# Query features in a linear-attention and FFN kernel: the eighth head pair in the empty rows of the seven others, the seventh pair in one group of 64x64 tiles

## The chip, the cores and the metric

The kernel runs on one core of one Trainium2 chip. The metric is the device time of one execution in microseconds (us). PE is TensorE, PEld its weight loads, ACT is ScalarE, DVE is VectorE, POOL is GpSimd and SP is SyncE, which issues most DMAs. A pair `p` of sequence tiles is 256 rows (there are 8: `NPAIR`); a head pair is two of the 16 heads (also 8).

## The reference

One layer norm feeds a linear attention with softmax feature maps and a SiLU FFN; both are added to the input. The sequence has 2048 rows, the width is 448, there are 16 heads of 28 and the FFN is 1792 wide.

```python
xn = _layernorm(x, axis=-1)
return x + _A_ref(xn, A_wqkv, A_w_phi, A_wo) + _B_ref(xn, B_w1, B_w2)
...
q, k, v = qkv[0], qkv[1], qkv[2]
pq = jnp.einsum("bhsd,hdf->bhsf", q, w_phi)
pk = jnp.einsum("bhsd,hdf->bhsf", k, w_phi)
phi_q = jnp.concatenate([_softmax(pq, axis=-1), _softmax(-pq, axis=-1)], axis=-1)
phi_k = jnp.concatenate([_softmax(pk, axis=-1), _softmax(-pk, axis=-1)], axis=-1)
kv = jnp.einsum("bhsf,bhsd->bhfd", phi_k, v)
z  = jnp.einsum("bhsf->bhf", phi_k)
num = jnp.einsum("bhqf,bhfd->bhqd", phi_q, kv)
den = jnp.einsum("bhqf,bhf->bhq", phi_q, z)[..., None] + 1e-6
...
h = _silu(jnp.einsum("bsd,df->bsf", x, w1))
out = jnp.einsum("bsf,fd->bsd", h, w2)
```

## The kernel before

All work is recorded as operations of a small planner (`P.op`, `P.dma`), each with an estimated duration; `schedule` simulates the five engines and fixes for each the order of its instructions. Data dependencies become semaphore waits (a DMA has a semaphore of its own), `odeps` only fix an order on one engine. In the attention and output stages the order of PE is written out by hand in the list `chain`. All matmuls go out through two helpers, so the profile shows them under few lines: L446 (`mms`, matmuls), L459 (`trs`, transposes), L465 (`act`, all of ACT), L469 (`copy_dve`).

The contraction over 448 is cut into rows of 64: `contract` issues steps of two matmuls, one on array rows 0 to 63 and one on rows 64 to 127, into two neighbouring PSUM banks for the two sequence tiles; a first pass of 4 steps and a second pass of 3 steps, which begins after the first has ended.

The stages in order of time:

1. Layer norm, transposes of the normed input into `xnT`, and the first layer of the FFN for the first part of the sequence (`ffn1_single`, `ffn1_chunk`, SiLU on ACT), from 0 to about 41 us. In between `fold(kt)` (L795), for four row blocks `kt`, multiplies the query and key weights by `w_phi` into banks 6 and 7 and copies the result to `wqk_sb`, where each head pair has 56 columns and 8 columns of padding. For the queries the padding is set to zero by a POOL memset (L526).
2. Attention, pair by pair, 41 to 84 us. `k_macro(p)` (L877) computes key features (`pk_mm`, 14 matmuls), two exponentials of them on ACT (`exp_k`), the values (`v_mm`, banks 2 and 3, copied by DVE as `v_ev`), sums `Sk`, reciprocals `Rk` on DVE, and the product `phik`, mostly on POOL (L900). `q_group(ch, c)` (L922), one for each `p`, computes the query features of two head pairs (2c and 2c+1) for one half of the sequence (`ch`, 1024 rows) as 7 steps of 512 columns into banks 6 and 7. The output has 128 rows: 56 of the first head pair, 8 empty, 56 of the second, 8 empty. Two exponentials (`exp_q`, plus and minus) write them to `EqT`. `k_acc(p)` accumulates the key-value product in bank 4, in odd pairs from the third on, between the two passes of the q group.
3. The rest of FFN layer 1, the transposed key-value block `KVZ` (`kv_transpose`), and the first `q_products` (`U_mm`): for one pair of sequence tiles, each of the four column blocks `c` of `EqT`, rows 0 to 55 and 64 to 119, times `KVZ`.
4. From 93.5 us on, `out_pair(p)`: FFN layer 2 and the output projection into one pair of banks (`obank`), `q_products(p + 2)` and `q_divide(p + 2)` (DVE, L1016 to L1029; POOL, L1051) in between, then the store.

```python
        for p in range(NPAIR):
            k12, v12 = k_macro(p)
            q12 = q_group(p // 4, p % 4)
            if p > 1 and p % 2:
                chain += [k12[0], v12[0], k12[1], v12[1], q12[0], k_acc(p - 3), k_acc(p - 2), q12[1]]
            else:
                chain += [k12[0], v12[0], k12[1], v12[1][:2], q12[0], v12[1][2:], q12[1]]
```

The memory `EqT` holds `[128 rows, 4 column blocks c, 2 signs, 2 sequence tiles, 1024]`; the first of its blocks serves as scratch in stage 1.

Of the kernel before, what the change touches and what calls it, by code (L numbers as in the profile page):

```python
# [8 lines left out]
ACTF = mybir.ActivationFunctionType  # L9
# [323 lines left out]
def bass_parallel_sum__linear_kernel_hedgehog__dense_activation_silu__prompt_kernel(  # L333
# [11 lines left out]
    NT, NPAIR = S // 128, S // 256  # L345
    KF = 3
    FT = FF // 128
# [7 lines left out]
    with es:  # L355
# [6 lines left out]
        xnT = sb("xnT", [128, 8, NPAIR, 128], BF16)  # L362
        wqk_sb = sb("wqk_sb", [128, 4, 2, 8, 64], BF16)
# [56 lines left out]
        P = _Prog()  # L420
        UP, LO = slice(0, 64), slice(64, 128)

        def d_mm(n):
            return max(n * 0.4167 + 1.0, 55.0)
# [4 lines left out]
        def d_dve(n, mode=1):  # L429
            return n * 1.042 / mode + 150.0  # L430
# [4 lines left out]
        def d_pool(n, per=1.0):  # L435
            return n * per + 120.0
# [27 lines left out]
        def act(dst, src, func, name, table=None, scale=1.0):  # L464
            return P.op("act", d_act(_cols(src)), lambda e: e.activation(dst, src, func, scale=scale),  # L465
                        reads=[src], writes=[dst], table=table, name=name)

        def copy_dve(dst, src, name, dur):
            return P.op("dve", dur, lambda e: e.tensor_copy(dst, src), reads=[src], writes=[dst], name=name)  # L469

        def xb(par, k):
            return 3 if k == 3 else (k if par == 0 else 4 + k)

        def contract(jobs, n, first, last, name, sync=None):

            passes = ([((0, 0, UP), (1, 0, LO)), ((0, 1, UP), (1, 1, LO)), ((0, 2, UP), (1, 2, LO)), ((0, 3, UP), (1, 3, LO))],
                      [((0, 0, LO), (1, 0, UP)), ((0, 1, LO), (1, 1, UP)), ((0, 2, LO), (1, 2, UP))])
            prev, done = None, []  # L480
            for q, steps in enumerate(passes):
                ops = []
                for X, W, dsts, opens, wstat in jobs:
                    for i, step in enumerate(steps):
                        parts = []
                        for par, k, r in step:
                            xx, ww = X(r, xb(par, k)), W(r, k)
                            lhsT, rhs = (ww, xx) if wstat else (xx, ww)
                            parts.append((dsts[par], lhsT, rhs, first and opens and q == 0 and i == 0,
                                          last and q == 1 and i == len(steps) - 1))  # L490
                        ops.append(mms(parts, name, d_mm(n)))
                if q == 1:
                    for o in ops:
                        o.syncs.add(prev.id)
                prev = ops[-1]
                done.append(ops)
            return done
# [24 lines left out]
            P.op("pool", d_pool(16, 2.0), lambda e: e.tensor_copy(kvz1, mask2[:, None, :].broadcast_to([128, 8, 2])),  # L522
                 reads=[mask2[:]], writes=[kvz1], name="kvz1")

        qpad = wqk_sb[:, :, 0, :, 56:64]
        P.op("pool", d_pool(256, 0.9), lambda e: e.memset(qpad, 0.0), writes=[qpad], name="qpad")  # L526
        P.op("pool", d_pool(256, 0.9), lambda e: e.memset(wraw[:, :, 2 * D:], 0.0), writes=[wraw[:, :, 2 * D:]], name="wpad")
        def warm(n, cols=256):

# [245 lines left out]

        def exp_act(dst, src, scale, name):
            o = act(dst, src, ACTF.Exp, name, table="exp", scale=scale)
            for s in silus:
                if s.id not in o.deps:
                    o.odeps.add(s.id)  # L780
            exps.add(o.id)
# [13 lines left out]
        def fold(kt):  # L795
            bA, bB = banks[6], banks[7]
            for w in range(9):
                parts = []
                pairs = [(UP, 4, bA, 448)] if w == 0 else [(UP, (w - 1) % 4, bA, 56 * (w - 1))]
                if 1 <= w <= 7:  # L800
                    pairs.append((LO, w % 4, bB, 56 * (w - 1)))
                for r, g, bk, c in pairs:
                    parts.append((bk[:, c:c + 56], wT[r, w, 128 * kt:128 * kt + 128], BD[r, g, :], True, True))
                mms(parts, "fold_mm", 36.0)
            qk = wqk_sb[:, kt].rearrange("p s (c j) u -> p (s c) j u", j=2)
            for src, dst, eng in ((bA[:, 0:448], qk[:, :, 1, 0:56], "act"), (bB[:, 0:392], qk[:, 1:8, 0, 0:56], "dve"),
                                  (bA[:, 448:504], qk[:, 0, 0, 0:56], "act")):
                n = _cols(src)
                if n > 56:
                    src = src.rearrange("p (s u) -> p s u", u=56)  # L810
                if eng == "act":
                    act(dst, src, ACTF.Identity, "fold_ev")
                else:
                    copy_dve(dst, src, "fold_ev", d_dve(n))

        ev0, order0 = lnz_first()
        banks_ = iter((0, 2, 4, 0, 2, 4, 0, 2))
# [58 lines left out]

        def k_macro(p):  # L877
            sl = p % NEK
            kbk = 4 if p == 1 else 0
            k12 = proj(p, lambda r, k: wqk_sb[r, k, 1, :, 0:56], kbk, "pk_mm")  # L880
            kb = psum[:, kbk * 512:kbk * 512 + 1024].rearrange("p (t c) -> p t c", t=2)[:, :, 0:D]
            for s in range(2):
                exp_act(Ek[sl][:, :, s * D:(s + 1) * D], kb, 1.0 if s == 0 else -1.0, "exp_k")
            v12 = proj(p, lambda r, k: wv_sb[r, k, :], 2, "v_mm")
            vb = psum[:, 1024:2048].rearrange("p (t c) -> p t c", t=2)[:, :, 0:D].rearrange("p t (h d) -> p t h d", h=H)
            copy_dve(vaug[sl][:, :, :, 0:DH], vb, "v_ev", d_dve(896))
            for t0, t1 in ((0, 2),) if p < NPAIR - 1 else ((0, 1), (1, 2)):
                n = t1 - t0
                E4 = Ek[sl][:, t0:t1, 0:2 * D].rearrange("p t (h f) -> p t h f", f=DH)
                S3, R3 = Sk[:, sl, 32 * t0:32 * t1], Rk[:, sl, 32 * t0:32 * t1]  # L890
                S4, R4 = (a.rearrange("p (t h) -> p t h", t=n) for a in (S3, R3))
                P.op("dve", d_dve(896 * n), lambda e, S4=S4, E4=E4: e.tensor_reduce(S4, E4, AXL.X, ALU.add),  # L892
                     reads=[E4], writes=[S3], name="Sk")
                P.op("dve", d_rec(32 * n), lambda e, S3=S3, R3=R3: e.reciprocal(R3, S3), reads=[S3], writes=[R3], name="Rk")
                for s0, s1, eng in ((0, 2, "pool"),) if t0 == 0 else ((0, 1, "dve"), (1, 2, "pool")):
                    h0, h1 = 16 * s0, 16 * s1
                    E5, R5 = E4[:, :, h0:h1], R4[:, :, h0:h1]
                    R5 = R5[:, :, :, None].broadcast_to([128, n, h1 - h0, DH])
                    P.op(eng, 1100 if eng == "dve" else d_pool(448 * n * (s1 - s0), 1.72),
                         lambda e, E5=E5, R5=R5: e.tensor_tensor(E5, E5, R5, ALU.mult),  # L900
                         reads=[E5, R5], writes=[E5], name="phik")

            return k12, v12
# [16 lines left out]
            return ops  # L920

        def q_group(ch, c):  # L922
            done = contract([(lambda r, b: xnT[r, b, 4 * ch:4 * ch + 4, :].rearrange("p a c -> p (a c)"),
                       lambda r, k: wqk_sb[r, k, 0, 2 * c:2 * c + 2, :].rearrange("p j u -> p (j u)"),
                       [banks[6 + par] for par in range(2)], True, True)], 512, True, True, "pq_mm")
            src = psum[:, 6 * 512:8 * 512].rearrange("p (r c) -> p r c", r=2)
            for s in range(2):
                exp_act(EqT[:, c, s, :, ch * 512:(ch + 1) * 512], src, 1.0 if s == 0 else -1.0, "exp_q")
            return done

        for sl in range(NEK):
            P.op("pool", d_pool(32), lambda e, sl=sl: e.memset(vaug[sl][:, :, :, DH], 1.0),
                 writes=[vaug[sl][:, :, :, DH]], name="vaug1")
        P.cur_prio = 0
        chain = []
        for p in range(NPAIR):
            k12, v12 = k_macro(p)
            q12 = q_group(p // 4, p % 4)
            if p > 1 and p % 2:
                chain += [k12[0], v12[0], k12[1], v12[1], q12[0], k_acc(p - 3), k_acc(p - 2), q12[1]]  # L940
            else:
                chain += [k12[0], v12[0], k12[1], v12[1][:2], q12[0], v12[1][2:], q12[1]]
        kv = k_acc(NPAIR - 2) + k_acc(NPAIR - 1)
        ready = [o.id for o in P.ops if o.name == "phik"][-2:]
        for o in kv:
# [39 lines left out]
        U4 = psum[:, UB * 512:UB * 512 + 2048].rearrange("p (q c) -> p q c", q=4)[:, :, 0:480].rearrange("p q (h c) -> p q h c", c=DZ)  # L985

        def obank(p):
            return 6 if p % 2 == 0 else 0

        def q_products(p):  # L990
            for t in range(2):
# [133 lines left out]

        unit_no[0] = 0
        k = len(units_done)
        ffn1_chunk(4, 2, 12, FT, (0,))
        unit_no[0] = 0
        ffn1_chunk(6, 2, 0, FT, (2, 6, 0, 6, 0, 6, 0))  # L1130
        u = units_done[k:]
        uu = []
        for p in range(2):
# [128 lines left out]
```

## Time and profile before

| | |
|---|---|
| three timed runs | 157.41, 156.87, 156.2 us (median 156.87) |
| profiled execution, its own time | 156.01 us |
| its span, first to last instruction | 154.3 us |
| PE busy | 149.6 us (97%) |
| DVE, ACT, POOL busy | 99.6, 75.7, 55.0 us |
| granted TensorE clock | 0.998 |
| q matmuls (64x512) | 112, 14.8 us busy |
| exponentials into EqT | 16 of 1.02 us |

A line of the chain of waits or of the timeline gives the start in us, the length in us, the engine, the line of the source and the number of instructions; a line of the waits gives who waited for whom, us in total, times, and the longest. The busy time of PE includes the modelled tail of each matmul, so costs of steps are read from the starts of consecutive groups.

### The profile page before, as it was taken

What the parts mean: (1) busy time and instruction counts of PE and PEld (TensorE: products, weight loads), DVE (VectorE), ACT (ScalarE), POOL (GpSimd) and SP (SyncE); (2) the same over time, 40 slices, a digit from 0 to 9 for tenths busy, and PEclk for the clock granted to TensorE, in tenths of its full rate; (3) what the DMA queues carried; (4) which work ended last, traced back from release to release, by engine and by line L of the source; (5) the groups of instructions that cost most, each with busy time, mean ns of one, the idle gap of its engine ahead of it and who ended that gap; (6) DMA issues with size and microseconds to landing.
All of it is one profiled execution on the core that took longest, in us unless ns stands there. A gap on an engine that the chain in (4) does not pass through costs nothing.

```text
span 154.3 us, 5662 instructions
## 1 busy us (share of the span) xinstructions
PE 149.6 (97%) x2576; PEld 98.9 (64%) x2576; DVE 99.6 (65%) x177; ACT 75.7 (49%) x89; POOL 55.0 (36%) x79
## 2 busy tenths in 40 slices
PE   6999999999998999999999999999999999999992
PEld 4698889898743445454478886645565555555672
DVE  1969788862427989494994597675665748393203
ACT  3586775569779886869869566021020202022000
POOL 7021123020100788858395024642516060605000
PEclk9999999999999999999999999999999999999999
DMA  4967754000004331210000000001101010101012
GB/s 129 339 190 185 256 170 130 4 4 4 4 0 121 123 119 59 79 44 0 4 0 4 4 0 6 4 0 64 46 18 59 0 64 0 64 2 64 0 64 60
DMA packets 8629, 9.60 MB, mean 62 GB/s; under 512 B 1501, under 2 KB 8221, under 8 KB 8605
## 3 DMA queue, kind: packets, MB, share of 16 engines
q1 hardware_dynamic: 8140, 8.96, 18.6%
q8 instruction: 20, 0.33, 0.9%
q10 hardware_dynamic: 464, 0.28, 0.6%
q14 instruction: 5, 0.03, 0.1%
HBM read 7.37 MB, written 1.84 MB: 60 GB/s over the span
## 4 chain that ended last, share of the span: by engine, by line
PE 94%; ACT 3%; issue 1%; POOL 0%; DVE 0%; ACTq 0%; POOLq 0%
PE psum L446 90%; PE psum L459 3%; ACT EqT L465 1%; ACT L465 1%; ACT scr L465 1%; ACT xnT L465 0%; DVE out_sb L1080 0%; POOL ident L501 0%; PE psum L967 0%; POOL ones_bf L500 0%; POOL neghalf L504 0%; ACTq L1202 0%; POOLq L1247 0%; POOL ones L505 0%
## 5 line engine op out<-in xcount | busy, mean ns | idle before, releaser
L446 PE MATMUL psum<-xnT,w_sb 64*128 64x256 bf16 (+1 forms) x768 | 46.8, 268 | 0.1
L446 PE MATMUL psum<-w_sb,hT 64*128 64x448 bf16 (+2 forms) x504 | 46.6, 328 | 0.0
L446 PEld LDWEIGHTS psum<-xnT,w_sb 64*128 64x128 bf16 x768 | 35.3, 94 | 5.2 <-PE psum L446 0.7
L465 ACT ACTIVATE hT<-psum 128x1024 bf16<-128x1024 f32 (+1 forms) x29 | 28.3, 995 | 13.8 <-PE psum L446 13.2
L1051 POOL TENSOR_TENSOR xn_sb<-wraw 128x448 bf16<-128x448 f32 (+4 forms) x39 | 20.7, 562 | 37.0 <-DVE wraw L1029 37.0
L446 PEld LDWEIGHTS psum<-w_sb,hT 64*128 64x128 bf16 x504 | 22.7, 94 | 16.6 <-ACT oT L465 0.4
L465 ACT ACTIVATE oT<-psum 128x896 bf16<-128x896 bf16 x8 | 7.3, 917 | 40.4 <-PE psum L459 40.4
L900 POOL TENSOR_TENSOR scr<-scr,Rk 128x1792 bf16<-128x1792 bf16 x6 | 19.3, 3211 | 18.0 <-ACT scr L465 11.3
L465 ACT ACTIVATE EqT<-psum 128x1024 bf16<-128x1024 f32 x16 | 15.5, 1023 | 5.5 <-PE psum L446 5.5
L1029 DVE TENSOR_TENSOR wraw<-psum,Gq 128x1792 f32<-128x1792 f32 (+1 forms) x9 | 16.4, 1817 | 0.9
L446 PE MATMUL psum<-xnT,wqk_sb 64*128 64x512 bf16 x112 | 14.8, 378 | 0.4 <-ACT EqT L465 0.4
L1080 DVE TENSOR_TENSOR out_sb<-psum,x_sb 128x896 bf16<-128x896 f32 (+2 forms) x9 | 8.8, 981 | 9.5 <-PE psum L446 9.4
L1016 DVE RECIPROCAL R<-psum 128x64 f32<-128x64 f32 (+1 forms) x9 | 4.6, 512 | 14.9 <-PE psum L446 14.9
L446 PE MATMUL psum<-wv_sb,xnT 64*128 64x448 bf16 x112 | 14.0, 349 | 0.0
L446 PE MATMUL psum<-wo_sb,oT 64*128 64x448 bf16 (+2 forms) x126 | 13.6, 328 | 0.0
L446 PE MATMUL psum<-wqk_sb,xnT 64*128 64x448 bf16 x112 | 13.2, 349 | 0.0
L607 DVE BATCH_NORM_STATS2 st<-x_sb 128x6 f32<-128x448 bf16 x16 | 9.8, 615 | 4.4 <-DMA x_sb<-in_A_x_dram 4.4
L892 DVE TENSOR_REDUCE Sk<-scr 128x64 f32<-128x1792 bf16 x6 | 12.1, 2013 | 0.6 <-ACT scr L465 0.6
L616 POOL TENSOR_TENSOR rstd<-ve,neghalf 128x2 f32<-128x2 f32 (+1 forms) x8 | 5.4, 670 | 19.6 <-DVE ve L615 19.6
L469 DVE CAST scr<-psum 128x896 bf16<-128x896 f32 x6 | 6.5, 1083 | 8.9 <-PE psum L446 8.9
L465 ACT ACTIVATE scr<-psum 128x896 bf16<-128x896 f32 x12 | 10.4, 922 | 0.7 <-PE psum L446 0.4
L446 PEld LDWEIGHTS psum<-xnT,wqk_sb 64*128 64x128 bf16 x112 | 4.7, 94 | 6.9 <-PE psum L446 1.7
(69 smaller groups left out, 139.6 us busy)
## 6 DMA issues: line engine op xcount, KB each, us to landing
out_dram<-out_sb SPq DMA_DIRECT2D x7, 224.0 KB, 1.9
w_sb<-in_B_w_dram SPq DMA_DIRECT2D x3, 448.0 KB, 3.3
x_sb<-in_A_x_dram SPq DMA_DIRECT2D x2, 448.0 KB, 4.3
w_sb<-in_B_w_dram SPq DMA_DIRECT2D x2, 384.0 KB, 7.2
x_sb<-in_A_x_dram SPq DMA_DIRECT2D x3, 224.0 KB, 6.1
w_sb<-in_B_w_dram SPq DMA_DIRECT2D x3, 224.0 KB, 3.3
wraw<-in_A_wqkv_dram SPq DMA_DIRECT2D x1, 672.0 KB, 4.8
w_sb<-in_B_w_dram SPq DMA_DIRECT2D x1, 576.0 KB, 4.2
```

The source lines that it names most:

```text
L446: r = e.matmul(dst, lhsT, rhs, start=start, stop=stop, skip_group_check=True)
L459: out = e.transpose(dst, src, ident[r, 64:128] if r == LO else ident[r, 0:64])
L465: return P.op("act", d_act(_cols(src)), lambda e: e.activation(dst, src, func, scale=scale), reads=[src], writes=[dst], table=table, name= ...
L469: return P.op("dve", dur, lambda e: e.tensor_copy(dst, src), reads=[src], writes=[dst], name=name)
L607: P.op("dve", 600, lambda e: e.bn_stats(st6[:, t, :], x_sb[:, t, :]), reads=[x_sb[:, t, :]], writes=[st6[:, t, :]], name="bnst")
L616: P.op("pool", 580, lambda e: e.tensor_tensor(r2, v2, nh, ALU.pow), reads=[v2, nh], writes=[r2], name="rstd")
L892: P.op("dve", d_dve(896 * n), lambda e, S4=S4, E4=E4: e.tensor_reduce(S4, E4, AXL.X, ALU.add), reads=[E4], writes=[S3], name="Sk")
L900: lambda e, E5=E5, R5=R5: e.tensor_tensor(E5, E5, R5, ALU.mult),
L1016: P.op("dve", d_rec(32 * n), lambda e, R3=R3, U=U: e.reciprocal(R3, U[:, :, :, DH + 1]), reads=[U[:, :, :, DH + 1]], writes=[r2], name="R2")
L1029: P.op("dve", d_dve(896 * n), lambda e, dsto=dsto, U=U, G3=G3, n=n: e.tensor_tensor(dsto, U[:, :, :, 0:DH], G3[:, :, :, None].broadcast_to ...
L1051: lambda e, dst=dst, a0=a0, a1=a1: e.tensor_tensor(dst, a0, a1, ALU.add),
L1080: P.op("dve", d_dve(2 * (c1 - c0)), lambda e: e.tensor_tensor(dst, ob, xs, ALU.add), reads=[ob, xs], writes=[dst], name="out_ev")
```

## The change

The zero padding of the query weights goes. In `fold`, the 56 query columns of the eighth head pair are also copied, 8 at a time, into the 8 padding columns of the seven other head pairs, and the copies of the fold change engines. So every q product now yields, in the 8 rows that were empty, 8 of the eighth pair's features.

Six `q_group`s remain (three for each half of the sequence, head pairs 0 to 5). In pair 3 a new `q_half` computes the seventh head pair for both halves of the sequence at once: each step has four matmuls on 64x64 tiles, two row halves times two halves of the sequence, the latter in rows 0 to 63 and 64 to 127 of the output. Pair 5 has no q group. DMAs within SBUF (`q_move`, issued on SP) then bring the features where `q_products` reads them: one of 56 rows (224 KB) and fourteen of 8 rows (32 KB each).

The banks of the q and k products in some pairs, of two FFN units and of the output pairs change; a dummy exponential (`pre_exp`) is placed after the last SiLU ahead of the attention's exponentials; the last four `Sk`/`Rk` operations get a fixed order.

As built, the order of instructions changes on PE also in the fold: 32, 24 (of them 2 a little later) and 24 FFN matmuls of 256 columns stand between the folds, and more behind the last. On SP two of the DMAs stand ahead of the three loads of `wo`, thirteen behind them and ahead of the stores. The first `U_mm` of the fourth column block waits for 7 DMA semaphores in pair 0 and for 8 in pair 4.

```diff
-        qpad = wqk_sb[:, :, 0, :, 56:64]
-        P.op("pool", d_pool(256, 0.9), lambda e: e.memset(qpad, 0.0), writes=[qpad], name="qpad")
...
         def exp_act(dst, src, scale, name):
             o = act(dst, src, ACTF.Exp, name, table="exp", scale=scale)
+            o.odeps.add(pre_exp.id)
...
-            for src, dst, eng in ((bA[:, 0:448], qk[:, :, 1, 0:56], "act"), (bB[:, 0:392], qk[:, 1:8, 0, 0:56], "dve"),
-                                  (bA[:, 448:504], qk[:, 0, 0, 0:56], "act")):
+            for src, dst, eng in ((bA[:, 0:448], qk[:, :, 1, 0:56], "dve"), (bB[:, 0:392], qk[:, 1:8, 0, 0:56], "act"),
+                                  (bA[:, 448:504], qk[:, 0, 0, 0:56], "dve")):
...
+            copy_dve(wqk_sb[:, kt, 0, 0:7, 56:64], bA[:, 168:224].rearrange("p (g u) -> p g u", u=8), "fold_ev", d_dve(56))
...
-            kbk = 4 if p == 1 else 0
+            kbk = {1: 4, 2: 6, 6: 6, 7: 6}.get(p, 0)
...
         def q_group(ch, c):
+            qb = {1: 0, 2: 4, 5: 0, 6: 0}.get(4 * ch + c, 6)
...
-                       [banks[6 + par] for par in range(2)], True, True)], 512, True, True, "pq_mm")
-            src = psum[:, 6 * 512:8 * 512].rearrange("p (r c) -> p r c", r=2)
+                       [banks[qb + par] for par in range(2)], True, True)], 512, True, True, "pq_mm")
+            src = psum[:, qb * 512:(qb + 2) * 512].rearrange("p (r c) -> p r c", r=2)
...
+        def q_half():
+            qb, done = 6, []
+            for q in range(2):
+                ops = []
+                for k in range(KF + 1 - q):
+                    parts = []
+                    for h, r in enumerate((UP, LO)):
+                        t = h if q == 0 else 1 - h
+                        for ch in range(2):
+                            parts.append((banks[qb + t][64 * ch:64 * ch + 64, :], wqk_sb[r, k, 0, 6, :],
+                                          xnT[r, xb(t, k), 4 * ch:4 * ch + 4, :].rearrange("p a c -> p (a c)"),
+                                          q == 0 and k == 0, q == 1 and k == KF - 1))
+                    ops.append(mms(parts, "pq_mm", d_mm(512), 65))
+                done.append(ops)
+            for o in done[1]:
+                o.syncs.add(done[0][-1].id)
+            src = psum[:, qb * 512:(qb + 2) * 512].rearrange("p (r c) -> p r c", r=2)
+            for s in range(2):
+                exp_act(EqT[:, 3, s, :, 0:512], src, 1.0 if s == 0 else -1.0, "exp_q")
+            return done
+
+        def q_move(dp, sp, n, c, dch, sch, name):
+            dst = EqT[dp:dp + n, 3, :, :, dch * 512:dch * 512 + 512]
+            src = EqT[sp:sp + n, c, :, :, sch * 512:sch * 512 + 512]
+            P.dma(lambda e: e.dma_start(out=dst, in_=src), n * 4096, reads=[src], writes=[dst], name=name)
+
+        def q_last(ch):
+            for g in range(6):
+                q_move(64 + 8 * g, 56 + 64 * (g % 2), 8, g // 2, ch, ch, "q_last")
...
+        pre_exp = act(pre[:, 1:2], neghalf[:, 0:1], ACTF.Exp, "pre", "exp")
+        pre_exp.odeps.update(o.id for o in silus)
+        exps.add(pre_exp.id)
...
-            q12 = q_group(p // 4, p % 4)
-            if p > 1 and p % 2:
+            q12 = []
+            if p == 3:
+                q12 = q_half()
+                q_move(112, 120, 8, 3, 1, 0, "q_last")
+                q_move(0, 64, 56, 3, 1, 0, "q_half")
+                q_move(112, 56, 8, 3, 0, 0, "q_last")
+                q_last(0)
+            elif p != 5:
+                q12 = q_group(p // 4, p % 4 - (p > 5))
+            if p == NPAIR - 1:
+                q_last(1)
+            if p == 5:
+                chain += [k12[0], v12[0], k12[1], v12[1], k_acc(2), k_acc(3)]
+            elif p > 1 and p % 2:
...
+        sums = [o for o in P.ops if o.name in ("Sk", "Rk")][-4:]
+        for a, c in zip(sums, sums[1:]):
+            c.odeps.add(a.id)
...
-            return 6 if p % 2 == 0 else 0
+            return 0 if p % 2 == 0 else 6
...
-        ffn1_chunk(4, 2, 12, FT, (0,))
+        ffn1_chunk(4, 2, 12, FT, (6,))
...
-        ffn1_chunk(6, 2, 0, FT, (2, 6, 0, 6, 0, 6, 0))
+        ffn1_chunk(6, 2, 0, FT, (2, 0, 6, 0, 6, 0, 6))
```

## The prediction

> **What bounds the kernel now.** I read the page's head first, then the chain that ended last, then the waits of TensorE (PE), then the timeline of the attention middle (41 to 84 us), which is where the change lies.
>
> ```profile
> span 154.3 us, 5662 instructions
> ...
> PE 149.6 (97%) x2576; PEld 98.9 (64%) x2576; DVE 99.6 (65%) x177; ACT 75.7 (49%) x89; POOL 55.0 (36%) x79
> ...
> PE 94%; ACT 3%; issue 1%; POOL 0%; DVE 0%; ACTq 0%; POOLq 0%
> ...
> PE psum L446 <- POOL ones L505: 1.4, 1, 1.4
> PE psum L446 <- ACT EqT L465: 0.4, 1, 0.4
> ```
>
> PE is busy 97% of the span and owns 94% of the chain that ended last. Its matmuls have two idle spells that the waits name: 1.4 us at the start, and 0.4 us behind an exponential into EqT. So only two things are worth time: matmul steps taken off PE, and that 0.4 us. The chain shows where the second comes from:
>
> ```profile
> 44.02 1.28 ACT L465
> ...
> 45.31 0.89 ACT scr L465 x2
> ...
> 46.92 1.96 ACT EqT L465 x2
> ...
> 48.93 36.54 PE psum L446 x496
> ```
>
> Between 44.0 and 48.9 the chain runs through ScalarE (ACT): its table load (1.28 us), exp_k of pair 0, exp_q of pair 0, and then PE again. The second q group needs banks 6 and 7, which exp_q of pair 0 is still reading. The next lines give the price of one q group and of a change of tile shape:
>
> ```profile
> 57.55 1.03 PE L446 MATMUL psum<-xnT,wqk_sb 64*128 64x512 bf16 x8
> ...
> 58.51 0.98 PE L446 MATMUL psum<-scr 128*58 128x112 bf16 x32
> ...
> 59.41 0.82 PE L446 MATMUL psum<-xnT,wqk_sb 64*128 64x512 bf16 x6
> ...
> 60.07 0.92 PE L446 MATMUL psum<-wqk_sb,xnT 64*128 64x448 bf16 x8
> ...
> 62.53 1.03 PE L446 MATMUL psum<-xnT,wqk_sb 64*128 64x512 bf16 x8
> ...
> 63.39 0.35 PE L446 MATMUL psum<-wv_sb,xnT 64*128 64x448 bf16 x2
> ```
>
> The printed length of a group includes the pipeline's tail, so I take starts. At 62.53 eight matmuls (four steps of two row halves) hold PE until 63.39: 0.86 us, 0.215 us for a step of 512 columns, or 0.42 ns a column.
>
> **The change part by part.**
>
> *Fewer steps.* Before, eight q groups take 7 steps each, 56 in all. After, six groups of that kind remain (42 steps), and q_half takes 7 steps of four 64x64 tiles for the seventh head pair in both halves of the sequence. The eighth pair's 56 features ride in the 8 empty columns of each of the seven others and cost no step. If four tiles take one step's time, 7 steps go: 7 x 0.215 = 1.50 us, all from the bounding engine. No row of before has four tiles at once. The neighbours are two: the q steps run two row halves together, and the kv matmuls (58.51) run two column halves together: 32 of 112 columns one after the other would be 32 x 47 ns = 1.49 us, and they take 0.90. Bounds for the seven steps: 0.215 us each (four together), 0.43 (two together: gain 0), 0.86 (one by one: 3.0 us lost). I take 0.215, since both kinds of pairing are in the trace and their product is what is asked for. The Trainium skill, "TensorE: Matmul & The Clock Gate", section "Part 3: Packing small matmuls — row/col tiling", gives about 4 ns for each further tile of a pack; by that the seven steps would take 7 x 3 x 4 ns = 0.08 us more, an estimate that no run here shows.
>
> *The idle spell.* After, the second q group takes banks 0 and 1, which exp_k of pair 0 left at 47.04, so PE need not wait at 48.5: 0.40 us. The table load is also pulled forward by a dummy exponential that follows the last silu (end 42.91) instead of waiting for the first k product; exp_k would start at 42.91 + 1.28 + 0.2 = 44.4 instead of 45.31. That alone would also free bank 6 before 48.5, so the two edits are worth 0.40 together, not 0.40 each. Bounds 0.3 and 0.41.
>
> *Changes of tile shape.* At 58.51 PE goes from 64x128 tiles to 128x64. Four steps from 57.55 end at 58.41, so the change costs 0.10; the way back costs 0.90 - 16 x 0.047 = 0.15. Today this is one round trip in each odd pair from the third on. With q_half, pair 3 goes 64x128, 64x64, 128x64, 64x64, 64x128: two changes more, 0.10 to 0.15 each. I take 0.20; bounds 0 (the row halves are kept) and 0.50. The Trainium skill says the same as the row in "TensorEngine Tiling (Array Packing)", section "Key Properties": changing the mode drains the array, changing the tile does not. By that rule all four changes of pair 3 are paid in full, and the trace agrees for the two that it has.
>
> *Waits on the copies.* U_mm of the fourth column block now reads rows brought by DMA: 7 semaphores at the first pair, 8 more at the fifth. If they are long met, only the queue's handling counts. For fold_mm at 32 us PE passes four DMA semaphores with no gap in its starts (bound 0); ACT's queue takes about 0.07 us around one wait (43.95 to 44.02 in the chain), 15 x 0.07 = 1.0 us as the other bound. I take 0.10, near the PE row. Queued behind them are the remaining U_mm and FFN matmuls, and DVE's q_divide waits for those.
>
> *Are they met?* In pair 3 the last exp_q ends at 62.2 (60.28 + 1.94). Fifteen DMAs follow on SP: two, then wo's three loads, then thirteen. A 32 KB copy inside SBUF is in the trace:
>
> ```profile
> xnT<-xnT SPq DMA_DIRECT2D x1, 32.0 KB, 2.2
> ```
>
> Its issue took 0.60 us on SP. Two chained landings (the 224 KB copy at about 3.3 us, as loads of 448 KB have it, then 2.2) and nine issues of 0.6 end near 73; the first U_mm stands at 86.55. The last six follow exp_q of the last pair (about 81): 6 x 0.6 + 2.2 ends near 87; their first reader is pair 4's U_mm, after 105. SP's own queue: wo's loads stay near 63.4 behind two issues (wo is read at 96.5), the first store comes at 103.5. Cost 0; without that cover PE would stand for the whole lateness.
>
> *Fold.* ACT keeps one copy per fold (392 columns) and DVE gets 448, 56 and 56 columns: about 0.62 + 0.2 + 0.2 = 1.0 us, from the 392-column CAST (0.57) and short DVE rows (0.19). Between folds PE now has 32, 24 and 24 FFN matmuls: at 84 in 4.5 us (78.84 on) that is 1.7, 1.3 and 1.3 us. With 0.2 us of start-up DVE ends just in time for the second and third. I take 0.05; bounds 0 and 0.4. The FFN matmuls that moved are run later, not added.
>
> *Nothing on the path.* Two exp_q fewer on ACT (2.0 us) are hidden behind PE. Pair 5 loses its q group, so v to v shrinks by 1.5 us there; DVE needs 1.09 + 2.01 + 0.55 = 3.65 us a pair and stood idle 2.18 us before v_ev of pair 6, which falls to about 0.7. The order Sk, Rk, Sk, Rk in the last pair helps little: POOL's phik of pair 6 ends at 80.22 and its last two then need 2.98, to 83.2, whatever DVE does; PE arrives at about 83.5. The mirrored banks (0 for 6) move no wait.
>
> *Sum.* -1.50 - 0.40 + 0.20 + 0.10 + 0.05 = -1.55 us. The profiled execution took 156.01 us, 1.7 more than its span of 154.3; the span should become 152.7 and that execution 154.5. The three timed runs are 157.41, 156.87 and 156.2; the mean with the profiled one is 156.6, so I put the time at 155.1.
>
> **The rivals.**
> *Two tiles at a time.* The row halves stream together but the column halves of a 64x64 step take turns: 14 x 0.215 us, the step gain is gone, the rest nets to about -0.05: 156.5. For it: no row has four. Against it: kv_mm's column halves, each with a stream of its own, do overlap. Pair 3 would then show 3.0 us of q. Stalls of 0.4 us at each of the three folds would lead to about the same place, 156.
> *One at a time (slower).* In pair 3 the 28 matmuls run one after the other: 28 x 0.215 = 6.0 us in place of the two removed groups' 3.0, so 3.0 lost and 0.05 won: 159.6. It decides from a step of 0.43 us on, above which the change loses. Against it: both overlaps above.
> *Late copies (slower).* PE stands at the first U_mm of column block 3 until the 8-row copies land. It wins the gain back from a landing near 86.6 us on and costs 1 us for each us more; at 6.9 us per landing (the slowest into EqT) and chained twice, plus issues, the copies still end near 82, so it takes more than the trace shows; priced at 158.
>
> **How the numbers follow.** Forecast 0.80. About 1% is what a measurement of this kernel can tell from no change (its runs spread 0.8%), 1.57 us, and my 1.55 us lies on that line: with the shape changes and waits at their low ends the gain is 1.9, at 0.50 and 0.4 it is 1.0, and the median of before stands above the profiled run, which tips it to 0.52 over the line and 0.28 under. Two at a time or fold stalls 0.08 (within 1%), one at a time 0.07 and late copies 0.05 (slower). Faster 0.52, same 0.36, slower 0.12. Range: 153.8 (gain 1.9 and the low runs) to 157.0 (two at a time, and half of what lies above no gain).
>
> **What would show it.** Right: the q_half groups of pair 3 take 0.86 and 0.65 us by starts, plus 0.1 to 0.15 at each change; no PE wait at 48.5; the DMA copies land ten or more us before U_mm; PE busy falls by about 1.5 us. Wrong: q_half at 3 us or more, PE waits named fold (L446 behind DVE wqk_sb), or a gap in front of U_mm.

## The result and the profile after

The changed kernel takes 154.73 us (median of four runs, 154.48 to 154.95) against 156.66 us before (156.2 to 157.41). The ratio is 0.9879, 95% interval 0.9842 to 0.9916: about 1.2% faster. The prediction had put the time at 155.1 us. In a second comparison of five rounds (last section of the experiments) the ratio is 0.9859, 0.9819 to 0.9899; two slow runs of the kernel before (159.69 and 160.02 us, granted clock 0.989) are left out of it. The profiled execution took 154.69 us with a span of 153.0, against 156.01 and 154.3 before.

The head of the changed kernel's page, and the waits of its matmuls (us in total, times, longest):

```profile
span 153.0 us, 5687 instructions
...
PE 148.3 (97%) x2576; PEld 98.2 (64%) x2576; DVE 100.5 (66%) x185; ACT 73.6 (48%) x84; POOL 54.7 (36%) x78
...
PE 91%; DMA 3%; ACT 1%; DVE 1%; SPq 1%; POOL 0%; issue 0%; POOLq 0%
```

```profile
PE psum L446 <- POOL ones L505: 1.4, 1, 1.4
...
PE psum L446 <- DVE xnT L469: 0.3, 1, 0.3
```

PE still bounds the kernel, with the same number of matmuls (the 28 on 64x64 tiles replace 28 of the old form) and 1.3 us less busy time. The wait behind the exponential into EqT is gone. A wait behind the eviction into `xnT` is new, and the chain that ended last now passes through a load of `x`. That piece lies in front of everything that the change touches:

```profile
12.51 5.33 DMA x_sb<-in_A_x_dram
...
17.86 0.63 DVE st L605
18.49 0.53 DVE xnT L469
...
19.07 2.60 PE psum L446 x44
```

DVE stood at the statistics of a tile whose load landed at 17.84, and the eviction that PE needed next was queued behind it. As far as the profiles show, it is not the change's work: a later run of the kernel before, whose one edit lies behind 41 us, waits there for 0.6 us, and a second profile of the changed kernel does not wait there at all. It matters for the reading, since it puts this execution 0.44 us behind that of before where PE leaves the transposes of the weights to be folded (31.01 against 30.57). So I cut the comparison at the first key matmul of pair 0 (41.69 before, 42.07 after): from there to the start of the last copy into `out_sb` (151.61 and 150.29) it is 109.92 us before and 108.22 after, 1.70 us less. The stretch repeats to 0.01 us in the second profile of the changed kernel (41.62 to 149.84), where the front differs by 0.45.

The timeline of PE before, at the places that the readings below compare (start, length, instructions):

```profile
41.69 0.92 PE L446 MATMUL psum<-wqk_sb,xnT 64*128 64x448 bf16 x8
...
66.37 0.73 PE L446 MATMUL psum<-wv_sb,xnT 64*128 64x448 bf16 x6
...
69.45 0.92 PE L446 MATMUL psum<-wqk_sb,xnT 64*128 64x448 bf16 x8
...
86.55 0.41 PE L446 MATMUL psum<-KVZ,EqT 56*128 56x60 bf16 x16
86.78 0.84 PE L446 MATMUL psum<-xnT,w_sb 64*128 64x256 bf16 x12
```

The same places and those of the change in the timeline of PE after:

```profile
42.07 0.92 PE L446 MATMUL psum<-wqk_sb,xnT 64*128 64x448 bf16 x8
...
48.37 0.54 PE L446 MATMUL psum<-wv_sb,xnT 64*128 64x448 bf16 x4
48.74 1.03 PE L446 MATMUL psum<-xnT,wqk_sb 64*128 64x512 bf16 x8
...
57.45 1.06 PE L446 MATMUL psum<-xnT,wqk_sb 64*64 64x512 bf16 x16
...
59.34 0.84 PE L446 MATMUL psum<-xnT,wqk_sb 64*64 64x512 bf16 x12
60.12 0.93 PE L446 MATMUL psum<-wqk_sb,xnT 64*128 64x448 bf16 x8
...
66.42 0.73 PE L446 MATMUL psum<-wv_sb,xnT 64*128 64x448 bf16 x6
...
67.98 0.93 PE L446 MATMUL psum<-wqk_sb,xnT 64*128 64x448 bf16 x8
...
84.07 1.05 PE L446 MATMUL psum<-xnT,w_sb 64*128 64x256 bf16 x16
85.00 0.65 PE L446 MATMUL psum<-KVZ,EqT 56*128 56x60 bf16 x16
85.47 0.83 PE L446 MATMUL psum<-xnT,w_sb 64*128 64x256 bf16 x12
```

At 48.37 four value matmuls (two steps, 0.37 us) run and the second q group follows at once. At 57.45 sixteen 64x64 matmuls hold PE for 0.99 us until the kv matmuls at 58.44, where eight 64x128 matmuls held it for 0.96. From 66.42, the second pass of pair 5's values, to the next key matmul it is 1.56 us, where before, with a q group in between, it was 3.08 (66.37 to 69.45). And the first U_mm group lasts 0.47 us by its starts (85.00 to 85.47) where it lasted 0.23 (86.55 to 86.78).

### The profile page after: what moved, and what is told of

Same layout as the page of the kernel before. It is cut to its first block, busy times and chain, and to the rows that moved or that the text cites. A ratio compares the mean times of both kernels' runs of the same rounds, so it can differ in the third digit from the quotient of the medians.

```text
span 153.0 us, 5687 instructions
## 1 busy us (share of the span) xinstructions
PE 148.3 (97%) x2576; PEld 98.2 (64%) x2576; DVE 100.5 (66%) x185; ACT 73.6 (48%) x84; POOL 54.7 (36%) x78
## 4 chain that ended last, share of the span: by engine, by line
PE 91%; DMA 3%; ACT 1%; DVE 1%; SPq 1%; POOL 0%; issue 0%; POOLq 0%
PE psum L446 88%; DMA x_sb<-in_A_x_dram 3%; PE psum L459 3%; ACT hT L465 1%; SPq L536 1%; DVE st L605 0%; ACT xnT L465 0%; DVE xnT L469 0%; DVE out_sb L1133 0%; POOL ident L501 0%; PE psum L1020 0%; POOL ones_bf L500 0%; POOL neghalf L504 0%; POOLq L1300 0%; POOL ones L505 0%
## 5 line engine op out<-in xcount | busy, mean ns | idle before, releaser
L465 ACT ACTIVATE EqT<-psum 128x1024 bf16<-128x1024 f32 x14 | 13.6, 1021 | 4.4 <-PE psum L446 4.3
L446 PE MATMUL psum<-xnT,wqk_sb 64*128 64x512 bf16 (+1 forms) x112 | 13.0, 379 | 0.0
L446 PEld LDWEIGHTS psum<-wo_sb,oT 64*128 64x128 bf16 x126 | 5.9, 94 | 4.8 <-ACT oT L465 0.2
```

Source lines behind the costliest of these rows:

```text
L446: r = e.matmul(dst, lhsT, rhs, start=start, stop=stop, skip_group_check=True)
```

## The experiments

Times between groups of matmuls are compared from one profile each, since they repeat to a few hundredths; the whole runs also carry the chance of the first loads.

**Column halves in separate steps.** Is the gain the four tiles in one step's time?

```diff
-                for k in range(KF + 1 - q):
...
-                        for ch in range(2):
+                for ch in range(2):
+                  for k in range(KF + 1 - q):
```

> The changed kernel with q_half in 14 steps of two 64x64 tiles (one column half at a time) in place of 7 steps of four. Theory (the gain is the number of steps, four tiles in one step's time): 7 steps of 0.215 us come back, +1.50 us; in pair 3 the first pass holds PE for 8 x 0.215 + 0.13 = 1.85 us up to the kv matmuls (0.99 with four tiles), the second 6 x 0.215 + 0.12 = 1.41 us (0.78). Rival (column halves take turns anyway, and the gain is from the idle spell and the first loads): the two passes stay near 0.99 and 0.78 us and the time does not move.

It lost nothing: 154.43 us, ratio 0.9881 (0.9813 to 0.9949), and 108.26 us from the first key matmul of pair 0 to the last copy. The first pass in the timeline of this kernel:

```profile
57.14 1.08 PE L446 MATMUL psum<-xnT,wqk_sb 64*64 64x512 bf16 x16
58.15 0.98 PE L446 MATMUL psum<-scr 128*58 128x112 bf16 x32
```

The program has eight matmuls on one column half and then eight on the other, and yet all sixteen take 1.01 us. The expected 1.50 us did not come back; the numbers are those of the expectation's rival, but its reason, that the column halves take turns, would need eight steps of 0.216 us, 1.73 us, for this pass. By this run alone another rival could also stand, that a 64x64 matmul needs half the time. The next run tells them apart.

**All on one column half.** The same matmuls in the same order as in the change, but with both halves of the sequence on the same tiles:

```diff
-                            parts.append((banks[qb + t][64 * ch:64 * ch + 64, :], wqk_sb[r, k, 0, 6, :],
+                            parts.append((banks[qb + t][0:64, :], wqk_sb[r, k, 0, 6, :],
```

> The changed kernel with all 28 matmuls of q_half on one column half of the array (both halves of the sequence write rows 0 to 63 of the banks, so the seventh head pair's features of the second half are left out and its output is not the reference's). Theory (tiles run beside each other as soon as they are different tiles, whatever the order of the program, so the run with the column halves in separate steps changed nothing; on the same tiles the steps must take turns): first pass 8 x 0.216 + 0.13 = 1.86 us to the kv matmuls, second 6 x 0.216 + 0.13 = 1.43, together 1.51 us more than the changed kernel. Rival (a 64x64 matmul of 512 columns takes half the time of a 64x128 one, so two tiles are enough): passes stay near 0.99 and 0.78.

```profile
57.69 1.92 PE L446 MATMUL psum<-xnT,wqk_sb 64*64 64x512 bf16 x16
59.54 0.97 PE L446 MATMUL psum<-scr 128*58 128x112 bf16 x32
60.45 1.49 PE L446 MATMUL psum<-xnT,wqk_sb 64*64 64x512 bf16 x12
61.86 0.93 PE L446 MATMUL psum<-wqk_sb,xnT 64*128 64x448 bf16 x8
```

The passes take 1.85 and 1.41 us, as expected, and the stretch from pair 0 on 109.73 us (42.31 to 152.04), 1.51 more than the change. So a step of two 64x64 matmuls costs 0.216 us, as one of two 64x128 matmuls does. What runs side by side is the two column halves, and without that the step gain is gone. The run before then says more: different tiles overlap although eight matmuls of one half stand in the program ahead of the other's first.

**The two edits of the idle spell, each alone in the kernel before.** The first is the dummy exponential:

```diff
             o = act(dst, src, ACTF.Exp, name, table="exp", scale=scale)
+            o.odeps.add(pre_exp.id)
...
+        pre_exp = act(pre[:, 1:2], neghalf[:, 0:1], ACTF.Exp, "pre", "exp")
+        pre_exp.odeps.update(o.id for o in silus)
+        exps.add(pre_exp.id)
```

> The kernel before with one thing of the change alone: the dummy exponential that pulls the table load ahead. Theory (PE's stall at 48.5 us is 0.57 us by the starts of the groups, of which the profile's idle time shows 0.40 since the modelled tails of the matmuls before cover the rest; each of the two edits alone removes it): from the first k matmul of pair 0 to the first q matmul of pair 1 6.67 us in place of 7.24, exp_k of pair 0 starts right behind the dummy. Rival (the early table gives only part, bank 6 is still read by exp_q of pair 0 when PE comes): 6.8 to 7.0.

The second is the banks:

```diff
-            kbk = 4 if p == 1 else 0
+            kbk = {1: 4, 2: 6}.get(p, 0)
...
+            qb = {1: 0, 2: 4}.get(4 * ch + c, 6)
```

> The kernel before with the other edit alone: the q group of pair 1 in banks 0 and 1, k of pair 2 in 6 and 7, q of pair 2 in 4 and 5. Theory: the same 6.67 us from the first k matmul of pair 0 to the first q matmul of pair 1, with exp_k of pair 0 still late (1.4 us behind the end of the last SiLU, as before); nothing is won by having both. Rival (the late ACT then holds up the next bank): a wait of 0.2 to 0.5 us turns up in pair 2.

The timeline with the early table alone:

```profile
42.13 0.92 PE L446 MATMUL psum<-wqk_sb,xnT 64*128 64x448 bf16 x8
...
48.42 0.54 PE L446 MATMUL psum<-wv_sb,xnT 64*128 64x448 bf16 x4
48.80 1.03 PE L446 MATMUL psum<-xnT,wqk_sb 64*128 64x512 bf16 x8
```

It is 6.67 us from 42.13 to 48.80; with the banks alone it is 6.67 from 41.29 to 47.96, and pair 2 shows no new wait. Both stretches to the last copy are 109.34 us, 0.58 less than before. Each edit removes the whole stall; having both adds nothing.

**No copies.** The DMAs of `q_move` are left out.

> The changed kernel without its fifteen DMAs inside SBUF, so the features of the last two head pairs are not put in place (one memset on POOL fills the rows that would stay unwritten). Theory (the seven semaphores, long met, cost PE 0.24 us in front of the first U_mm of column block 3): the first group of 16 U_mm goes from 0.47 back to 0.23 us by starts, and the span loses 0.24 us. Rival (the 0.24 us are something of U_mm itself, such as the new place of the banks): the group stays at 0.47 us. The eight waits of pair 4 cost nothing in the changed kernel's trace, so nothing is expected there.

The first U_mm group is back at 0.24 us (84.80 to 85.04), and the stretch is 107.98 us (41.87 to 149.85), 0.24 less. So the copies cost 0.24 us, all of it there.

**The same copies, waited for earlier.** PE passes the seven semaphores one at a time ahead of FFN matmuls:

```diff
         u = units_done[k:]
+        early_moves = [o.id for o in P.ops if o.name in ("q_last", "q_half")][2:9]
+        for o, d in zip(u[2][0] + u[1][1], early_moves):
+            o.deps.add(d)
```

> The changed kernel with the same copies, but PE passes the seven semaphores one by one in front of seven earlier FFN matmuls (third FFN unit after the last q group, from about 79.7 us on). Theory (it is the handling of seven waits in a row while PE's queue is empty, not the landing of the copies): first group of U_mm at 0.23 us, FFN matmuls at their 0.107 us a pair, span 0.24 us less than the changed kernel's for the same first 41 us. Rival (the copies land late or wait for each other): the FFN matmuls stop instead, nothing is won.

```profile
84.32 0.40 PE L446 MATMUL psum<-KVZ,EqT 56*128 56x60 bf16 x16
84.56 0.82 PE L446 MATMUL psum<-xnT,w_sb 64*128 64x256 bf16 x12
```

The group takes 0.24 us, the 84 FFN matmuls ahead of the kv product 4.68 (4.67 with the change), and the stretch is 107.98 us (41.39 to 149.37). The copies had therefore landed when PE passed the waits, which in this run's trace stand on weight loads up to 79.7 us; what cost 0.24 us was seven waits in a row at that place. In whole runs it is 154.3 us, ratio 0.9877 (0.9813 to 0.9941): too small to be seen there.

The trace of the change shows how the 0.24 us come about. These are the weight loads (PEld) of the first U_mm group:

```profile
85.00 0.14 PEld L446 LDWEIGHTS psum<-KVZ,EqT 56*128 56x128 bf16 x6 [0.16 <-ACT KVZ L465]
85.30 0.23 PEld L446 LDWEIGHTS psum<-KVZ,EqT 56*128 56x128 bf16 x10 [0.16 <-issue]
```

PE has just waited for `KVZ`, and six weight loads go at once. The seventh, the first of column block 3, comes 0.30 us later. In between, the trace records three semaphore instructions of PE's sequencer, at 85.01, 85.12 and 85.23 us, each for two of the seven semaphores; the last semaphore stands on the weight load itself. So one such instruction takes about 0.11 us, and the six short U_mm ahead cover only the first. The eight waits of pair 4 stand in front of the same U_mm, behind six of 60 columns as well, and cost nothing: the sequencer passes seven of them in four instructions from 109.28 to 109.66 us, while the U_mm start only at 110.77, behind matmuls that are still running. By these rows what decides is how far the sequencer is ahead of the matmuls, and right behind a real wait it is not ahead.

**Four of the seven early.** The same list cut with `[:4]`.

> The changed kernel with four of the seven semaphores passed early, three left in front of the first U_mm of column block 3. Theory (each wait costs PE the same, 0.24 / 7 = 0.034 us): the first group of 16 U_mm takes 0.24 + 3 x 0.034 = 0.34 us by starts. Rival (any wait there costs the whole 0.24, since it is the stop that costs and not the number): 0.47.

```profile
85.08 0.43 PE L446 MATMUL psum<-KVZ,EqT 56*128 56x60 bf16 x16
85.34 0.83 PE L446 MATMUL psum<-xnT,w_sb 64*128 64x256 bf16 x12
```

Neither: 0.26 us. Three waits cost 0.03 at most, seven cost 0.24, so the price is not the same for each, nor is it the stop itself. The trace fits the semaphore instructions: with three waits one is left (85.09 us) and the weight load follows at 85.16. Two instructions fewer at 0.11 us are the 0.21 us by which the group is shorter than with seven. No other number of waits was run.

**Both passes of q_half joined.**

```diff
+            elif p == 3:
+                chain += [k12[0], v12[0], k12[1], v12[1], q12[0], q12[1], k_acc(0), k_acc(1)]
```

> The changed kernel with both passes of q_half one behind the other and the kv matmuls behind them: three changes of tile shape in pair 3 in place of four, but nothing between the passes. Theory (about 0.12 us for each change; the second pass waits for the end of the first, whose tail is about 0.17 us): from the first q matmul to the next pair's first k matmul 2.67 us now, minus 0.12, plus 0.1 to 0.2, so 2.6 to 2.75. Rival (changes between 64x128 and 64x64 are free, the 0.24 us more is something else): 2.8 to 2.9.

```profile
57.21 1.97 PE L446 MATMUL psum<-xnT,wqk_sb 64*64 64x512 bf16 x28
59.11 0.98 PE L446 MATMUL psum<-scr 128*58 128x112 bf16 x32
60.02 0.93 PE L446 MATMUL psum<-wqk_sb,xnT 64*128 64x448 bf16 x8
```

It is 2.81 us from 57.21 to 60.02 against 2.67 with the change, which is the rival's number, but the weight loads show another reason: those of the second pass begin at 58.34, 1.13 us behind the first pass's first matmul, where four steps need 0.86. The wait between the passes is 0.27 us, not 0.1 to 0.2, and 2.67 - 0.13 + 0.27 = 2.81 with one change of shape fewer. So I keep the price of a change, read from the change's own starts and weight loads below; the run doesn't show it by itself.

**A version that beats both.** The early waits, and the statistics of tile 8 behind the eviction that PE needs:

```diff
-        later4 = [o for o in P.ops[k:] if o.eng == "dve"][2:]
+        later4 = [o for o in P.ops[k:] if o.eng == "dve"]
```

> The changed kernel with the seven semaphores passed early and the statistics of sequence tile 8 put behind the eviction of pair 3's transposes on DVE. Theory (the 0.2 to 0.8 us that some executions lose near 19 us come from DVE standing at the load of that tile with PE's next input queued behind it, in either kernel): PE no longer waits for DVE xnT near 19 us, the spread of the timed runs shrinks, and the median lies 0.3 to 0.6 us under the changed kernel's in these rounds. Rival (the planner's new order of the first 31 us costs as much): within 0.2 us of the early-waits kernel.

> The kernel with the seven semaphores passed early once more, in more rounds, beside the changed kernel. Theory: 0.24 us less than the changed kernel from pair 0's first k matmul to the end (110.6 to 110.7 us in place of 110.9), about 0.2 us in the median, which lies inside the spread that the first loads make. Rival: no difference in that stretch.

> The changed kernel as it is, beside the other two. Theory: 154.3 to 154.9 us, a ratio of 0.985 to 0.992 to the kernel before; 110.9 us from pair 0's first k matmul to the end (112.6 before), whatever the first loads do.

| | runs, us | median | ratio to before (95%) |
|---|---|---|---|
| statistics behind, early waits | 153.59 to 154.06 | 153.82 | 0.9812 (0.978 to 0.9844) |
| early waits | 153.99 to 154.35 | 154.21 | 0.9836 (0.9804 to 0.9867) |
| the change | 154.19 to 155.69 | 154.22 | 0.9859 (0.9819 to 0.9899) |

The first is 0.40 us under the change in the median, and its slowest run is faster than the change's fastest. Its one profile has no wait of PE for the eviction into `xnT`, but neither have the profiles of the other two in this comparison; those wait near 5.5 us (and the early waits once more at 9.4) for DVE's normalized rows, 0.7 us with the change and 0.9 in all with the early waits, ahead of the place that the edit moves. So the profiles do not show the edit at work. From pair 0 on it takes 107.98 us, as the early waits do (107.97 here); by the medians its further gain lies in the front. The early waits alone did not lower the median: the 0.25 us that they save behind 41 us were used up in front of it (41.96 to the first key matmul, 41.62 with the change). What in the front gives the first one its gain, the place of the statistics or the planner's other order of the first 31 us, is not shown.

## Why the prediction was right, term by term

The sum was -1.55 us; on the stretch from pair 0 on the change gave -1.70 and with the fold -1.76. The first loads took back 0.44 of it in the profiled pair, so the spans differ by 1.3. The medians differ by 1.93; what goes beyond 1.76 is not shown to be the change's. The two largest errors, a stall taken 0.17 too small and waits taken 0.14 too small, nearly cancel, so part of the closeness of the sum is luck. The terms below add up to -1.69 on the stretch, which leaves 0.01 for the mirrored banks and the order of `Sk` and `Rk`, neither of which was run alone. The low end of the range, 153.8 us, does not follow from its own terms: a gain of 1.9 and the lowest run of before (156.01) make 154.1.

| term | predicted | measured, us | from |
|---|---|---|---|
| seven steps | -1.50 | -1.52 | 3.08 to 1.56 around pair 5; one column half +1.51 |
| idle spell | -0.40 | -0.57 | 7.24 to 6.67, either edit alone too |
| changes of shape | +0.20 | +0.24 | 0.09 ahead of q_half, 0.03 and 0.12 behind its passes |
| waits on copies | +0.10 | +0.24 | first U_mm group 0.23 to 0.47 |
| fold | +0.05 | -0.06 | 30.57 to 41.69, 31.01 to 42.07 |
| start of the first U_mm | none | -0.08 | 85.54 to 86.55, 84.07 to 85.00 |

*Steps.* Right in mechanism and size. The rivals with two tiles or one at a time are out: by starts the passes take 0.99 and 0.78 us, and the run on one column half shows what they would have cost.

*Idle spell.* Right in place, mis-sized by 0.17 us and outside its bounds of 0.3 to 0.41. The sum took the idle time that the wait's line shows, but the profile counts the modelled tail of the last value matmuls as busy. By starts, two steps of 0.187 us from 47.98 end at 48.35, and PE went on at 48.93: 0.58. I had read steps by starts for just that reason and did not do so for the stall. The two edits are worth one stall together, as the step said.

*Changes of shape.* The trace of the change has four in pair 3: 0.10, 0.13, 0.15 and 0.13 us, each the time left when the streaming is taken off. Before, the two of that pair were 0.10 and 0.15. The rule of the Trainium skill, "TensorEngine Tiling (Array Packing)", section "Key Properties", that a change of mode drains the array, agrees: going from 64x128 to 64x64, with the row halves kept, costs as much as the others. That it is the shape and not the semaphore wait at the head of each group shows in the weight loads of the change. A plain q group also waits for ACT there, but its loads begin 0.18 us ahead of its first matmul (52.77 and 52.95) and no time is lost; the loads of a new shape begin only with the matmuls (57.45 and 58.44), after an idle time of 0.37 and 0.41 us.

*Waits.* The term that was most wrong for its size: 0.24 us in place of 0.10. In the row of before that I leaned on (four semaphores in the fold, no gap) PE's sequencer passed them at 31.54 and 31.65 us, ahead of the weight load that needs them (31.88), while FFN matmuls ran. In front of the U_mm PE had just waited for `KVZ` and had next to nothing ahead. The eight waits of pair 4 cost nothing: one round of the output stage takes 7.29 us there, as before.

*Late copies.* Out. The early waits held nothing up, the last of them at 79.7 us, more than 4 us ahead of that run's U_mm (84.32). An issue took 0.69 us rather than the 0.60 of the sum, which the cover swallowed: with the change the last of the seven copies was issued by 71.7 us, 13 us ahead of the U_mm.

*Fold.* No stall, and 0.06 us less in place of 0.05 more, for which no cause is shown. DVE's three copies took 0.87 us in place of 1.0, and PE found banks 6 and 7 free. The old split of the copies between the engines wasn't tried in the changed kernel.

*Nothing on the path.* Right in outcome, but the working compared two times of before: POOL's last products ending at 83.2 us, PE arriving at 83.5. The change brings PE there at 82.05. It did not wait, because POOL's product of pair 6 began at 75.49 in place of 77.01 and the last two ended at 81.64. Had POOL stayed where the prediction left it, 1.2 us would have been lost; this step held by luck.

*Start of the first U_mm.* The -0.08 us were in no term. PE waits there for two copies into `KVZ`, of which ACT's ends last. Before, the trace has the wait for ACT as a semaphore instruction of its own (86.44 us), and the weight load follows 0.08 us later (86.52). After, the wait for DVE is the instruction (84.82) and the one for ACT stands on the weight load (85.00), 0.05 us behind the end of ACT's copy where it was 0.12. So the two waits changed places; no part of the change was meant to do that.

## What to carry to other kernels

When PE is busy all the way, count steps. Empty rows of an output and the other column half of the array are free places for work: a step of 512 columns cost 0.216 us here with two tiles or with four. Size a stall by the starts of the groups around it, not by the idle time of the profile. Do not put several semaphores that are long met in a row right behind a wait that PE really makes; put them earlier, one at a time, or where matmuls are still queued ahead. And compare two executions from the first common point behind the loads.

## What the hardware showed that I had not expected

Matmuls on different tiles do not keep to the program's order: with eight 512-column matmuls of one column half ahead of eight of the other, all sixteen took 1.01 us (0.99 when the halves alternate, 1.85 on one half). The Trainium skill, "TensorE: Matmul & The Clock Gate", section "Part 3: Packing small matmuls — row/col tiling", calls matmuls strictly first in, first out; this run does not agree. And seven waits that were long met cost 0.24 us right behind a real wait, where three cost 0.03 and eight, passed 1.1 us ahead of the matmuls, nothing; PE's sequencer took 0.11 us for a semaphore instruction with two of them.
